# Loading v in four gated pieces, and q and k in eight pieces issued between the GpSimd sums, in an attention-and-feed-forward kernel

## The chip, the cores and the metric

The kernel runs on one core of a Trainium2 chip. The metric is device time in microseconds. A pass is one round of the main loop, for one of the eight batches; passes and units are counted from 0.

## The reference, cut to what matters

Inputs are q, k and v of shape (8, 8, 576, 64): batch, heads, sequence, head dimension. For each batch, groups of 18 sequence positions of q and k are averaged to 32 landmarks. Three softmax matrices are built from q, k and their landmarks, one is inverted by six Newton steps, and the product with v gives the attention output. The result goes through `((x @ w1) * (x @ w2)) @ w3 @ w_out`.

```python
q_lm = q.reshape(B, H, m, S // m, D).mean(axis=3)      # m = 32
k_lm = k.reshape(B, H, m, S // m, D).mean(axis=3)
A, Bm, C = sm(q, k_lm), sm(q_lm, k_lm), sm(q_lm, k)
Z = ...                                                # six times: Z = 2 * Z - Z @ Bm @ Z
attn = A @ Z @ C @ v
```

## The kernel before

The order of instructions on each engine is the order of the program. In pass b of the main loop TensorE makes the eight "up" units of batch b, interleaved with the steps of `attention` for batch b+1, then the "down" products of batch b. Meanwhile batch b+2 is prepared: its q and k are transposed by DMA, and GpSimd makes the landmark sums (`landmarks`), which end in the tile `parts`. The first step of `attention` for batch b+2 reads `parts` at the very end of pass b. q and k of batch b+3 are loaded in the same pass by GpSimd; these loads cast float32 to float16.

```python
def load_qk(st, b):
    qkn = pin.tile([128, 2, H, 384], FP16, name="qkn")
    for t, src in ((1, k), (0, q)):
        nc.gpsimd.dma_start(out=qkn[0:NP, t, :, :],
                            in_=src[b].rearrange("h (p r) d -> p h (r d)", p=NP))
...
def landmarks(st, t, eng=nc.gpsimd):
    ...
        eng.tensor_tensor(out=tr, in0=x[:, :, 0, :], in1=x[:, :, 1, :], op=ALU.add)
        eng.tensor_tensor(out=tr, in0=tr, in1=x[:, :, 2, :], op=ALU.add)
        ...                                              # two adds of thirds to o
        eng.tensor_copy(out=hi, in_=o)                   # hi and lo are halves of st["parts"]
        eng.tensor_tensor(out=lo, in0=o, in1=hi, op=ALU.subtract)

def attention(st, bank=None):
    ...
    psL = small()
    for i in range(2):                                   # hi, then lo
        nc.tensor.matmul(psL[:, :], iit.rearrange("p a d -> p (a d)"),
                         parts[:, i].rearrange("p t h l -> p (t h l)"),
                         start=(i == 0), stop=(i == 1))
    ...

for b in range(B):
    st = sts[b]
    ab = st["ab"] = pab.tile([128, 8, S], FP16, name="ab")
    if b + 2 < B:
        turn_all(b + 2)                                  # DMA transposes of q and k
        load_v(sts[b + 2], b + 2)                        # one load on the SP queue
    ...
    for j in range(8):
        up(st, j, 0)
        ...
        steps(at, ...)
        up(st, j, 1)                                     # VectorE writes ab[:, j, :]
    if b + 3 < B:
        load_qk(sts[b + 3], b + 3)
    if b + 2 < B:
        landmarks(sts[b + 2], 1)
        landmarks(sts[b + 2], 0)
    nxt = attention(sts[b + 2], acc) if b + 2 < B else iter(())
    ...                                                  # down products, rest of at
    steps(nxt)                                           # TensorE reads parts of b + 2
    at = nxt
```

The softmax here doesn't subtract the row's maximum and nothing guards it: scores larger than these inputs give would overflow.

## Time and profile before

| | before |
|---|---|
| time, median | 300.87 us (299.02 to 301.57, 3 runs; 300.5 with the run made beside the changed kernel) |
| TensorE (PE) busy | 276.5 of 299.0 us |
| GpSimd (POOL) busy | 135.6 us |
| one pass of the loop (passes 1 to 5) | 26.6 to 30.5 us |

From the page: the span, the busy time of each engine, the granted TensorE clock in 40 slices (9 is 90% or more), and the chain that ended last by engine.

```profile
span 299.0 us, 9452 instructions
...
PE 276.5 (92%) x4026; PEld 151.7 (51%) x4026; DVE 177.9 (59%) x454; ACT 124.3 (42%) x199; POOL 135.6 (45%) x176
...
PEclk9998999999979999999999999999999999999999
...
PE 73%; DMA 9%; DVE 9%; ACT 6%; issue 2%; POOL 0%; ACTq 0%; DVEq 0%
```

TensorE is busy nearly all the time and makes up 73% of the chain. GpSimd is on none of it (0%): what it does is done in time. GpSimd's timeline in pass 2 (start in us, duration, engine, line, operation):

```profile
146.18 0.72 POOL L262 TENSOR_TENSOR bmbd<-bmn,mask 128x256 f32<-128x256 f32 x1
146.84 0.82 POOL L71 DMA_DIRECT2D qkn<-in_k_dram  x1
147.65 0.77 POOL L71 DMA_DIRECT2D qkn<-in_q_dram  x1
148.43 1.65 POOL L166 TENSOR_TENSOR tr<-qkT 128x768 f32<-128x768 f16 x1
150.16 1.64 POOL L167 TENSOR_TENSOR tr<-tr,qkT 128x768 f32<-128x768 f32 x1
...
160.04 0.67 POOL L175 TENSOR_TENSOR parts<-o,parts 128x256 f16<-128x256 f32 x1
```

After the last product of the attention steps (line 262) GpSimd issues the two q/k loads, 0.82 and 0.77 us, and goes straight into twelve adds and copies that end at 160.04 + 0.67 = 160.7 us. This is the timeline of TensorE at the psL matmuls of passes 0, 1 and 2, which read that result:

```profile
108.68 0.64 PE L183 MATMUL small<-parts,iit 128*128 128x512 f16 x2
...
137.45 0.59 PE L183 MATMUL small<-parts,iit 128*128 128x512 f16 x2
...
164.12 0.61 PE L183 MATMUL small<-parts,iit 128*128 128x512 f16 x2
```

In pass 2 TensorE comes for `parts` at 164.1 us, 3.4 us after they are ready; in pass 1 it comes 5.6 us after. In pass 0 there is nothing between: the sums end at 108.9 us.

### The profile page before, as it was taken

The page shows a single profiled execution, that of the slowest core. Times are in us where ns is not written, and L with a number is a line of the kernel's source. Part 1 is how long each engine was busy: PE and PEld are TensorE (multiplying, and loading weights), DVE is VectorE, ACT ScalarE, POOL GpSimd, SP SyncE. Part 2 cuts the span into 40 slices and gives each one's busy share as a digit, 9 for nine tenths or more (in the row PEclk, how much of TensorE's full clock was granted, in tenths as well). Part 3 has the DMA queues.
Part 4 walks back from the last instruction along what each step waited for, and adds up shares of the span by engine and source line. Part 5 has one row for each costly group of instructions (what it writes and reads, how often), then busy time and mean ns, then how long its engine had stood idle before and what let it go on. Part 6 is the DMA issues. An engine that isn't in the chain of part 4 may idle for free.

```text
span 299.0 us, 9452 instructions
## 1 busy us (share of the span) xinstructions
PE 276.5 (92%) x4026; PEld 151.7 (51%) x4026; DVE 177.9 (59%) x454; ACT 124.3 (42%) x199; POOL 135.6 (45%) x176
## 2 busy tenths in 40 slices
PE   6867999999879989999999998999999999999993
PEld 3434555444446447445744663366447535743741
DVE  8922743465476576755765765476666655765720
ACT  2113442233344266236625741474167236525531
POOL 1608132270009958950994499039918940600000
PEclk9998999999979999999999999999999999999999
DMA  6999999939920948975996999379949632013124
GB/s 242 279 268 255 239 232 230 164 38 196 203 54 8 214 110 172 224 165 104 186 219 150 147 201 202 101 140 203 228 111 154 154 107 70 4 30 79 36 58 118
DMA packets 61385, 45.56 MB, mean 152 GB/s; under 512 B 34976, under 2 KB 53408, under 8 KB 61344
## 3 DMA queue, kind: packets, MB, share of 16 engines
q1 hardware_dynamic: 46896, 31.86, 47.1%
q0 software_dynamic: 13632, 11.54, 24.8%
q10 hardware_dynamic: 816, 1.57, 1.4%
q8 instruction: 31, 0.51, 0.7%
q14 instruction: 10, 0.08, 0.1%
HBM read 38.80 MB, written 9.44 MB: 161 GB/s over the span
## 4 chain that ended last, share of the span: by engine, by line
PE 73%; DMA 9%; DVE 9%; ACT 6%; issue 2%; POOL 0%; ACTq 0%; DVEq 0%
PE big L426 16%; PE acc L446 13%; PE big L446 10%; PE acc L490 9%; DMA qkn<-in_q_dram 6%; PE big L412 6%; DVE ab L432 4%; PE big L369 4%; ACT a_sb L430 3%; DMA wof<-in_moe_w_out_dram 2%; PE small L305 2%; PE acc L305 2%; PE big L477 2%; PE big L353 1%; PE big L224 1%
## 5 line engine op out<-in xcount | busy, mean ns | idle before, releaser
L426 PE MATMUL big<-ahat,gt 128*128 128x288 f16 x512 | 75.1, 288 | 3.1 <-ACT a_sb L430 1.9
L432 DVE TENSOR_TENSOR ab<-a_sb,big 128x576 f16<-128x576 f16 x64 | 47.9, 750 | 19.5 <-PE big L426 7.7
L430 ACT CAST a_sb<-big 128x576 f16<-128x576 f32 x64 | 41.0, 640 | 41.6 <-PE big L426 36.1
L426 PEld LDWEIGHTS <-gt 128*128 128x128 f16 x512 | 47.6, 98 | 20.7 <-issue 5.8
L235 POOL TENSOR_TENSOR t<-ect 96x384 f32<-96x384 f32 x16 | 16.0, 997 | 87.0 <-ACT ect L228 86.5
L490 PE MATMUL acc<-wsp,w3t 128*128 128x512 f16 x168 | 42.1, 384 | 1.6 <-DVE wsp L471 0.9
L446 PE MATMUL acc<-w,ab 128*128 128x512 f16 (+1 forms) x192 | 41.0, 382 | 0.1
L446 PEld LDWEIGHTS <-ab 128*128 128x128 f16 (+1 forms) x320 | 23.9, 100 | 32.4 <-issue 9.3
L446 PE MATMUL big<-w,ab 128*128 128x512 f16 x128 | 32.8, 381 | 0.0
L166 POOL TENSOR_TENSOR tr<-qkT 128x768 f32<-128x768 f16 x14 | 23.0, 1643 | 20.7 <-DMA qkT<-qkn 11.0
L418 DVE TENSOR_SCALAR gt<-big 128x1024 f16<-128x1024 f32 x16 | 19.5, 1224 | 17.7 <-PE big L412 17.7
L490 PEld LDWEIGHTS <-w3t 128*128 128x128 f16 x192 | 18.1, 100 | 20.1 <-issue 4.1
L452 ACT ACTIVATE o_sb<-acc 128x512 f32<-128x512 f32 x20 | 11.9, 597 | 37.4 <-PE acc L446 35.5
L167 POOL TENSOR_TENSOR tr<-tr,qkT 128x768 f32<-128x768 f32 x14 | 23.0, 1641 | 1.1
L416 ACT ACTIVATE gt<-big 128x1024 f16<-128x1024 f32 x16 | 16.4, 1024 | 8.6 <-PE big L412 8.6
L412 PE MATMUL big<-wup,zt 64*32 64x512 f16 x512 | 19.0, 380 | 0.8 <-DVE ahat L356 0.8
L483 DVE SCALAR_TENSOR_TENSOR w3t<-big,w3t 128x512 f16<-128x512 f32 x16 | 11.0, 689 | 14.1 <-ACT w3t L482 14.1
L452 ACT ACTIVATE o_sb<-big 128x512 f32<-128x512 f32 x16 | 9.6, 598 | 22.4 <-PE big L446 22.4
L482 ACT ACTIVATE w3t<-big 128x512 f16<-128x512 f32 x16 | 9.5, 597 | 19.9 <-PE big L477 19.5
L228 ACT ACTIVATE ect<-big 96x768 f32<-96x768 f32 x16 | 12.9, 807 | 2.9 <-PE big L224 2.4
L356 DVE TENSOR_TENSOR ahat<-eat,big 128x576 f16<-128x576 f16 x16 | 11.9, 749 | 1.8 <-PE big L353 1.8
L172 POOL TENSOR_TENSOR o<-o,tr 128x256 f32<-128x256 f32 x14 | 11.2, 799 | 1.1
(311 smaller groups left out, 358.9 us busy)
## 6 DMA issues: line engine op xcount, KB each, us to landing
vt<-in_v_dram SPq DMA_DIRECT2D x8, 1152.0 KB, 8.5
qkn<-in_k_dram POOLq DMA_DIRECT2D x8, 576.0 KB, 10.8
qkn<-in_q_dram POOLq DMA_DIRECT2D x8, 576.0 KB, 13.4
out_dram<-o_sb SPq DMA_DIRECT2D x24, 192.0 KB, 2.3
w3f<-in_moe_w_dram SPq DMA_DIRECT2D x6, 512.0 KB, 7.5
out_dram<-o_sb SPq DMA_DIRECT2D x24, 128.0 KB, 2.4
wup<-in_moe_w_dram POOLq DMA_DIRECT2D x4, 512.0 KB, 24.9
wof<-in_moe_w_out_dram ACTq DMA_DIRECT2D x3, 512.0 KB, 7.3
```

Of the source, the lines that this page charges most:

```text
L166: eng.tensor_tensor(out=tr, in0=x[:, :, 0, :], in1=x[:, :, 1, :], op=ALU.add)
L167: eng.tensor_tensor(out=tr, in0=tr, in1=x[:, :, 2, :], op=ALU.add)
L235: nc.gpsimd.tensor_tensor(out=t3[0:NP], in0=e[:, :, 0:3, :], in1=e[:, :, 3:6, :], op=ALU.add)
L412: nc.tensor.matmul(psG[32 * h:32 * h + 32, qd, :], zt[rs, i, h, :], wup[rs, h, w, fs], start=(i == 0), stop=(i == 1), tile_position=(64 * ...
L416: nc.scalar.activation(out=g[:, :, w, fs], in_=psG, func=AXF.Copy, scale=1.0 / ZS)
L418: nc.vector.tensor_scalar(out=g[:, :, w, fs], in0=psG, scalar1=1.0 / ZS, scalar2=None, op0=ALU.mult)
L426: nc.tensor.matmul(p[:, c, 0:HS], st["g"][:, qd, w, 128 * j:128 * j + 128], st["ahat"][qd][:, c, :], start=(qd == 0), stop=(qd == 1))
L430: nc.scalar.copy(out=st["a_sb"], in_=p[:, :, 0:HS])
L432: nc.vector.tensor_tensor(out=st["ab"][:, j, :].rearrange("p (c s) -> p c s", c=2), in0=st["a_sb"], in1=p[:, :, 0:HS], op=ALU.mult)
L446: nc.tensor.matmul(pso[o:o + sz, :], ab[:, j, s0:s0 + sz], w34[:, j, :], start=(j == 0), stop=(j == 7), tile_position=(0, o))
L452: nc.scalar.activation(out=o_sb, in_=pso[:, :], func=AXF.Copy, scale=1.0 / (X64 * X64))
L490: nc.tensor.matmul(psW[j][:, :], turned[j, c // 4][:, a, c % 4, :], wsp[:, b, c, :], start=(c == 0 and a + b == 0), stop=(c == 7 and a == 1))
```

## The change

The aim is to spread the loads over the pass. v comes in four pieces of two heads, and each may start only when an up unit is done: a one-column GpSimd copy reads `ab` and writes into the v tile, so that the load has to wait for it. q and k come in eight pieces of two heads, their issues set between the GpSimd sums.

```diff
--- before.py
+++ after.py
@@ -77,6 +77,23 @@
         nc.sync.dma_start(out=vt[0:NP], in_=v[b].rearrange("h (p r) d -> p h (r d)", p=NP))
         st["vt"] = vt
 
+    def load_v_piece(st, b, i, done):
+        if i == 0:
+            st["vt"] = pin.tile([128, H, 384], FP32, name="vt")
+        hs = slice(2 * i, 2 * i + 2)
+        nc.gpsimd.tensor_copy(out=st["vt"][0:NP, 2 * i, 0:1], in_=done)
+        nc.sync.dma_start(out=st["vt"][0:NP, hs],
+                          in_=v[b, hs].rearrange("h (p r) d -> p h (r d)", p=NP))
+
+    def qk_pieces(st, b):
+        st["qkn"] = pin.tile([128, 2, H, 384], FP16, name="qkn")
+        for t, src in ((1, k), (0, q)):
+            for i in range(4):
+                hs = slice(2 * i, 2 * i + 2)
+                nc.gpsimd.dma_start(out=st["qkn"][0:NP, t, hs, :],
+                                    in_=src[b, hs].rearrange("h (p r) d -> p h (r d)", p=NP))
+                yield
+
     def load_weight(t, w):
         for qd in range(2):
             nc.gpsimd.dma_start(out=wup[64 * qd:64 * qd + 64, :, t, :],
@@ -155,7 +172,7 @@
         return mask4, par, ones, eye2, iit, onesq, selc, lomask
 
 
-    def landmarks(st, t, eng=nc.gpsimd):
+    def landmarks(st, t, eng=nc.gpsimd, pieces=iter(())):
         if "parts" not in st:
             st["parts"] = pz.tile([128, 2, 2, H, 32], FP16, name="parts")
         for h0 in ((0,) if eng is nc.gpsimd else (0, 4)):
@@ -163,13 +180,17 @@
             hs = slice(h0, h0 + n)
             x = st["qkT"][:, t, hs, :, :]
             tr = pat.tile([128, n, NP], FP32, name="tr" + own, bufs=1)
+            next(pieces, None)
             eng.tensor_tensor(out=tr, in0=x[:, :, 0, :], in1=x[:, :, 1, :], op=ALU.add)
+            next(pieces, None)
             eng.tensor_tensor(out=tr, in0=tr, in1=x[:, :, 2, :], op=ALU.add)
+            next(pieces, None)
             t3 = tr.rearrange("p h (l g) -> p h l g", g=3)
             o = pat.tile([128, n, 32], FP32, name="o3" + own, bufs=1)
             hi, lo = st["parts"][:, 0, t, hs, :], st["parts"][:, 1, t, hs, :]
             eng.tensor_tensor(out=o, in0=t3[:, :, :, 0], in1=t3[:, :, :, 1], op=ALU.add)
             eng.tensor_tensor(out=o, in0=o, in1=t3[:, :, :, 2], op=ALU.add)
+            next(pieces, None)
 
             eng.tensor_copy(out=hi, in_=o)
             eng.tensor_tensor(out=lo, in0=o, in1=hi, op=ALU.subtract)
@@ -596,7 +617,6 @@
         ab = st["ab"] = pab.tile([128, 8, S], FP16, name="ab")
         if b + 2 < B:
             turn_all(b + 2)
-            load_v(sts[b + 2], b + 2)
         if b % 2 == 0:
             chunks = [[(b, ab, 128 * t, 128)] for t in range(4)]
         else:
@@ -607,12 +627,13 @@
             if b == 0 and j == 1:
                 landmarks(sts[1], 0, nc.vector)
             steps(at, (0, 0, 0, 1, 1, 1, 2, 2)[j] if b == 0 else 1)
+            if b + 2 < B and j > 3:
+                load_v_piece(sts[b + 2], b + 2, j - 4, st["ab"][0:NP, j - 1, st.get("t0", 0):st.get("t0", 0) + 1])
             up(st, j, 1)
-        if b + 3 < B:
-            load_qk(sts[b + 3], b + 3)
         if b + 2 < B:
-            landmarks(sts[b + 2], 1)
-            landmarks(sts[b + 2], 0)
+            pieces = qk_pieces(sts[b + 3], b + 3) if b + 3 < B else iter(())
+            landmarks(sts[b + 2], 1, pieces=pieces)
+            landmarks(sts[b + 2], 0, pieces=pieces)
         nxt = attention(sts[b + 2], acc) if b + 2 < B else iter(())
         hold = {}
         nd = 2 * len(chunks)
```

The order of instructions on TensorE, VectorE and ScalarE is the same in both kernels; only the GpSimd and SP streams differ.

## The prediction

> **What bounds the kernel now.** TensorE. The page's busy table has PE at 276.5 of 299.0 us (92%), and the chain that ended last is 73% PE. From about 95 us the kernel runs one batch in 27 to 30 us (windows table: PE busy 28.1 of 28.8, 26.0 of 26.9, 28.4 of 30.1). No load is waited for there: the list of waits, restricted to 110 to 270 us, shows nobody waiting for v, q, k or their transposes. So spreading v and q/k over time has almost nothing to win; the only DMA wait in it is ACT for output stores, 1.9 us in two places.
>
> **What the change does to engines.** The instruction order on PE, ACT and DVE is unchanged. On GpSimd, each of six batches gets four one-column copies (the gates), and batches 0 to 4 issue eight q/k loads instead of two, threaded between the landmark sums. GpSimd is in order, so (1) the sums of batch b+2 cannot start before the last gate, which waits for `ab` of unit 6, and (2) the issues sit inside the chain of sums. That chain ends in `parts`, which PE reads (psL matmul, line 183) at the batch boundary. PE is in order too: if `parts` is late, PE stands.
>
> **Costs, from the timeline of GpSimd before.** One batch's sums take 12.3 us (119.60 to 131.89). A 768-row q/k issue occupies GpSimd 0.77 to 0.82 us; a 256-row weight issue still 0.63. The Trainium skill ("DMA: Bandwidth & Descriptors", section "SWDGE vs HWDGE vs iDMA") says a GpSimd core computes these descriptors in software; the trace agrees that issuing occupies the engine. A line through the two sizes gives, as an estimate, 0.6 us for a 192-row piece, so 4.9 us for eight against 1.6 before. A gate I put at 0.3 us (the existing one-column gate copy took 0.43).
>
> **Slack, from the timelines.** New end of sums = end of `ab` 6 + 0.35 + 12.3 + 4.9:
> - batch 0: before, sums end at 108.9 and PE reads at 108.7 to 109.3, zero slack. `ab` 6 is early (92.9), so the delay is gates 1.0 + issues 3.3 = 4.3 us.
> - batch 1: 122.5 + 17.5 = 140.0, needed 137.45: 2.6.
> - batch 2: 151.3 + 17.5 = 168.8, needed 164.1: 4.7.
> - batch 3: 178.2 + 17.5 = 195.7, needed 194.5: 1.3.
> - batch 4: 208.3 + 17.5 = 225.8, needed 221.2: 4.7.
> - batch 5: no pieces, 247.5 against 249.8: none.
>
> Sum 17.6 us, all on the critical path since PE has nothing else in its order. A stall shifts everything after it, so the stalls add up.
>
> **Prediction: 318 us, 309 to 325; faster 0.04, within 2% 0.11, slower 0.85.**
>
> **What would show it.** New waits PE small L183-equivalent <- POOL `parts`, about five, sum 13 to 22 us, longest 4 to 5 us; POOL busy up by about 20 us, with 40 q/k issue records of about 0.6 us; PE busy time unchanged; batches 0, 2 and 4 stretched by 4 to 5 us, 1 and 3 by less; v pieces landing well before use; nobody waiting for qkT.
>
> **What would make it wrong.** The piece issue cost decides. If it scaled with rows (0.2 us each), the stalls shrink to about 4 us in batches 0, 2 and 4 together, and the time to 305 (within 2%). If it did not shrink at all (0.8), the sum is about 25 us. If late q pieces hold the transposes at the next batch's start so long that sums wait for them, it is worse than 325. It would be faster only if TensorE matmuls are slowed by bursts of DMA in a way this trace does not list as a wait.

## The result, and the profile after

| | before | after |
|---|---|---|
| time, median of 4 | 300.5 us (299.02 to 301.57) | 319.61 us (318.58 to 320.1) |
| ratio | | 1.0635, 95% interval 1.058 to 1.069 |
| PE busy | 276.5 us | 283.5 us |
| POOL busy | 135.6 us | 156.4 us |

A ratio is the mean time of one kernel's runs over that of the other's of the same rounds, so it is not quite the ratio of the medians quoted. Executions over 1.5% slower than the fastest of the same kernel are left out of the means. The page after, the same lines, the second line of the chain (by line of the program), and a group that is new in the list of costly ones (in a group: busy us, mean ns, then the idle time of its engine just before it and what ended most of that):

```profile
span 316.8 us, 9556 instructions
...
PE 283.5 (89%) x4026; PEld 155.0 (49%) x4026; DVE 178.5 (56%) x454; ACT 124.9 (39%) x199; POOL 156.4 (49%) x230
...
PEclk9989999999799989997999799999986999999998
...
PE 47%; POOL 27%; DMA 8%; DVE 8%; issue 5%; ACT 4%; ACTq 0%; DVEq 0%; POOLq 0%
PE big L447 15%; PE acc L511 9%; POOL qkn L93 8%; DMA qkn<-in_q_dram 5%; POOL tr L186 5%; POOL tr L184 5%; PE acc L467 5%; DVE ab L453 4%; PE big L467 4%; POOL o L192 2%; DMA wof<-in_moe_w_out_dram 2%; PE big L433 2%; POOL o L191 2%; PE small L326 2%; ACT a_sb L451 2%
...
L204 PE MATMUL small<-parts,iit 128*128 128x512 f16 x16 | 6.6, 432 | 17.1 <-POOL parts L195 13.0
```

GpSimd now holds 27% of the chain, with the q/k issues (line 93) as its largest item, and TensorE waits 13.0 us for `parts`. The clock row has four slices at 7 or 6, where the row before had one. The timeline of GpSimd in pass 2 of the changed kernel:

```profile
151.88 0.73 POOL L283 TENSOR_TENSOR bmbd<-bmn,mask 128x256 f32<-128x256 f32 x1
...
157.13 0.18 POOL L84 CAST vt<-ab 96x1 f32<-96x1 f16 x1 [1.39 <-DVE ab L453]
157.37 0.69 POOL L93 DMA_DIRECT2D qkn<-in_k_dram  x1
158.07 1.65 POOL L184 TENSOR_TENSOR tr<-qkT 128x768 f32<-128x768 f16 x1
159.66 0.66 POOL L93 DMA_DIRECT2D qkn<-in_k_dram  x1
160.34 1.65 POOL L186 TENSOR_TENSOR tr<-tr,qkT 128x768 f32<-128x768 f32 x1
...
173.61 0.66 POOL L196 TENSOR_TENSOR parts<-o,parts 128x256 f16<-128x256 f32 x1
```

The last gate (line 84) waited for unit 6 until 157.1 us, 4.5 us after GpSimd had done everything else that came before it (151.88 + 0.73 = 152.6). Then each issue takes 0.66 to 0.69 us of GpSimd, and the sums end 16.9 us after the first issue began, where the two issues and the same sums took 13.9 us before (146.84 to 160.71). And the timeline of TensorE at the same matmuls as shown before; the number in brackets is its idle time and who ended it:

```profile
109.90 0.59 PE L204 MATMUL small<-parts,iit 128*128 128x512 f16 x1 [2.79 <-POOL parts L195]
...
141.54 0.38 PE L204 MATMUL small<-parts,iit 128*128 128x512 f16 x1 [1.46 <-POOL parts L195]
...
173.58 0.38 PE L204 MATMUL small<-parts,iit 128*128 128x512 f16 x1 [3.62 <-POOL parts L195]
174.33 0.38 PE L204 MATMUL small<-parts,iit 128*128 128x512 f16 x1 [0.37 <-POOL parts L196]
```

In pass 2 TensorE now stands 3.62 us for the first and 0.37 us for the second of the two matmuls. The five waits come to 13.0 + 1.4 = 14.4 us by the list of waits. To see the rest of the 19 us, take the interval from one start of the psB matmuls, just behind psL, to the next. The first interval ends behind the psL of pass 0, the next behind that of pass 1, and so on; the last has no q/k pieces in its pass and no wait at its end. "Fill" and "v on VectorE" are experiments told below.

| interval, us | 0 | 1 | 2 | 3 | 4 | 5 | sum |
|---|---|---|---|---|---|---|---|
| before | 23.3 | 28.8 | 26.6 | 30.5 | 26.6 | 28.8 | 164.5 |
| after | 27.5 | 31.2 | 32.2 | 32.1 | 31.2 | 30.2 | 184.4 |
| fill (e5) | 27.6 | 30.8 | 30.8 | 31.2 | 30.8 | 28.8 | 180.0 |
| v on VectorE (e12) | 23.6 | 28.8 | 26.6 | 28.8 | 26.6 | 28.8 | 163.0 |

Every interval that ends in a wait grew. Interval 3 grew by only 1.6 us, less than its wait of 1.9, because the kernel before had a standstill of 1.0 us of its own there (told under e12). Interval 5 grew by 1.4 us although nothing waits for `parts` in it. The windows table of the changed kernel behind the wait of pass 2 shows what may have done it (window, its length, PE busy and instructions, granted clock, DMA share, GB/s):

```profile
core 0: us, PE busy (x), PEclk, DMA share, GB/s
173.50:174.50 1.00, 0.55 (x2) 1.00 1.27 188
174.50:175.50 1.00, 1.00 (x5) 0.54 1.84 197
175.50:176.50 1.00, 1.00 (x13) 0.50 1.65 87
176.50:177.50 1.00, 1.00 (x6) 0.50 1.34 230
177.50:178.50 1.00, 1.00 (x14) 0.75 1.28 287
178.50:179.50 1.00, 0.92 (x8) 1.00 0.72 137
```

About a microsecond after the wait the granted clock falls to 0.50 for some 3 us. This is found behind four of the five waits, for 3 to 7 us; behind the fourth it stays at 1.00.

### The profile page after: what moved, and what is told of

Read it like the earlier page. It is cut to its first block, busy times and chain, and to the rows that moved or that the text cites. A ratio compares the mean times of both kernels' runs of the same rounds, so it can differ in the third digit from the quotient of the medians.

```text
span 316.8 us, 9556 instructions
## 1 busy us (share of the span) xinstructions
PE 283.5 (89%) x4026; PEld 155.0 (49%) x4026; DVE 178.5 (56%) x454; ACT 124.9 (39%) x199; POOL 156.4 (49%) x230
## 4 chain that ended last, share of the span: by engine, by line
PE 47%; POOL 27%; DMA 8%; DVE 8%; issue 5%; ACT 4%; ACTq 0%; DVEq 0%; POOLq 0%
PE big L447 15%; PE acc L511 9%; POOL qkn L93 8%; DMA qkn<-in_q_dram 5%; POOL tr L186 5%; POOL tr L184 5%; PE acc L467 5%; DVE ab L453 4%; PE big L467 4%; POOL o L192 2%; DMA wof<-in_moe_w_out_dram 2%; PE big L433 2%; POOL o L191 2%; PE small L326 2%; ACT a_sb L451 2%
## 5 line engine op out<-in xcount | busy, mean ns | idle before, releaser
L447 PE MATMUL big<-ahat,gt 128*128 128x288 f16 x512 | 80.9, 304 | 2.9 <-ACT a_sb L451 1.3
L447 PEld LDWEIGHTS <-gt 128*128 128x128 f16 x512 | 49.7, 103 | 25.2 <-issue 8.5
L84 POOL CAST vt<-ab 96x1 f32<-96x1 f16 x24 | 4.3, 182 | 42.1 <-issue 21.8
L204 PE MATMUL small<-parts,iit 128*128 128x512 f16 x16 | 6.6, 432 | 17.1 <-POOL parts L195 13.0
L211 DVE TENSOR_TENSOR qbd<-lm,par 128x512 f16<-128x512 f16 x8 | 5.5, 692 | 19.4 <-ACT lm L209 19.4
```

The source lines that it names most:

```text
L447: nc.tensor.matmul(p[:, c, 0:HS], st["g"][:, qd, w, 128 * j:128 * j + 128], st["ahat"][qd][:, c, :], start=(qd == 0), stop=(qd == 1))
```

## The experiments

The theory on trial: GpSimd time ahead of the end of the sums is the whole cost. The gates hold the sums back, the issues make them longer, both use up the same slack, and TensorE then waits and loses clock. Rivals: the pieces hurt as transfers, by landing late or by contention; or the two parts of the change cost something each, and add.

### e1: only the v pieces

```diff
-            pieces = qk_pieces(sts[b + 3], b + 3) if b + 3 < B else iter(())
-            landmarks(sts[b + 2], 1, pieces=pieces)
-            landmarks(sts[b + 2], 0, pieces=pieces)
+            load_qk(sts[b + 3], b + 3)          # whole, where they were before
+            landmarks(sts[b + 2], 1)
+            landmarks(sts[b + 2], 0)
```

> Only the gated v pieces; q and k go back to two whole loads ahead of the sums. Theory (GpSimd order: the sums start late because of the gate on unit 6, and grow by the issues between them, until they run past the slack before TensorE reads parts): the sums end 14.2 us after ab of unit 6 instead of 17.8, which is within the slack in batches 1 and 3, about 1.1 us past it in 2 and 4, about 0.4 in 0. So 2.6 us of waits for parts plus at most 2 for a lowered TensorE clock: 303.5 us, 301.5 to 305.5. Rival A (the pieces hurt as transfers: q/k landing late or contending with other transfers): q/k whole again, so before's time, 300.5, unless v is to blame. Rival B (the two parts of the change add up, the gate being the larger): 310 or more.

Measured: 302.09 us (301.52 to 303.22), ratio to before 1.003 (0.9992 to 1.0068). Its list of waits has 2.6 us for `parts`, as reckoned. The gates alone cost nothing that can be told from noise.

### e2: only the q/k pieces

```diff
         if b + 2 < B:
             turn_all(b + 2)
+            load_v(sts[b + 2], b + 2)
-            if b + 2 < B and j > 3:
-                load_v_piece(...)
```

> Only the q/k pieces between the sums; v is one ungated load as before. Theory: sums start when they did before and take 3.7 us longer (eight issues of 0.66 us against two of 0.80). Batch 0 had no slack: 3.7 us; batch 1 had 5.5 and batch 3 7.2: nothing; batches 2 and 4 had 3.4: 0.3 each. 4.3 us of waits plus about 1.7 of lowered clock: 306 us, 303.5 to 308. The two halves alone then make about 9 us of the 19: the rest is there only when both eat the same slack. Rival A (the pieces as transfers): close to the whole 319. Rival B (additive): 310.

Measured: 307.69 us (307.45 to 308.49) in three runs, a fourth, slow one of 312.29 left out; ratio 1.0229 (1.0189 to 1.0269). That is at the upper end of what was expected. The waits for `parts` were 2.9 us where 4.3 were reckoned; three other standstills, 3.9 us in all, were not reckoned: 1.0 us at 57 us, ahead of the loop, 2.4 in pass 1 and 0.6 in pass 3. The one in pass 1:

```profile
124.54 1.16 PE L447 MATMUL big<-ahat,gt 128*128 128x288 f16 x8
128.06 0.40 PE L390 MATMUL big<-sz__1715,tz__1716 32*32 32x96 f32 x16 [2.36 <-issue]
```

2.36 us pass with no releaser that the profile shows. In the weight loads the gap falls behind the first of the sixteen loads of this group, so nothing new was to be waited for. The queues of the DMA engines in the microsecond from 125 us, where it starts (packets, MB, share of 16 engines):

```profile
q0 software_dynamic: 147, 0.11, 72.0%
q1 hardware_dynamic: 66, 0.08, 40.9%
q8 instruction: 1, 0.02, 8.5%
```

An instruction block crosses just then, while q/k pieces and the whole v load fill the engines to 113% by this count. The Trainium skill ("Runtime: NRT & Kernel Launch", section "Instruction fetch mechanics") says that instructions are refilled in 16 KiB blocks by DMA while the engine works on the previous block, and calls the cost mostly hidden. Here it may not be hidden. e10 tests whether the whole v load has a part in it; what speaks against it is told under e9 and e12.

The two halves alone cost 1 and 7 us by the medians, together 19. So they do not add, and the reason is the slack: in passes 1 to 4 either half alone stays within it or passes it by little.

### e3: v pieces with their gates on VectorE

```diff
-        nc.gpsimd.tensor_copy(out=st["vt"][0:NP, 2 * i, 0:1], in_=done)
+        nc.vector.tensor_copy(out=st["vt"][0:NP, 2 * i, 0:1], in_=done)
```
(with e1's whole q/k loads)

> As the v-only kernel, but the one-column gate copies run on VectorE, just behind the ab that they wait for; v still arrives in four gated pieces. Theory: GpSimd is as before, so no wait for parts, and v in pieces wins nothing: 300.5 us, 299.5 to 302.5 (24 small copies on VectorE). Rival A (v pieces hurt as transfers or their issue blocks the output stores behind them): as the v-only kernel. Rival C (spreading v is a gain that the GpSimd cost hides): below 299.

Measured: 299.44 us (299.24 to 301.85), ratio 0.9967 (0.9919 to 1.0015). No wait for `parts` on GpSimd. With GpSimd left alone, v in pieces costs nothing, and may win a little; e12 says which.

### e4: GpSimd adds in the places of six issues

```diff
 def qk_pieces(st, b):
-    for t, src in ((1, k), (0, q)):
-        for i in range(4):
-            ... nc.gpsimd.dma_start(...)          # eight pieces
-            yield
+    load_qk(st, b)                               # two whole loads
+    yield
+    spare = pat.tile([128, 4, NP], FP32, name="trv", bufs=1)
+    for i in range(6):
+        nc.gpsimd.tensor_tensor(out=spare[:, :, 0:64], in0=selc[:, 0, :, 0:64],
+                                in1=selc[:, 0, :, 64:128], op=ALU.add)
+        yield
```

> The changed kernel with q and k as two whole loads and, in the places of the other six issues, six GpSimd adds of about 0.65 us that nobody reads. Theory (GpSimd time in the chain of sums is all that the pieces cost): as the changed kernel, 319.6 us, 317 to 322. Rival A (what costs is the pieces' transfers): as the v-only kernel, about 303.

Measured: 321.72 us (319.69 to 323.59), ratio 1.0687. The adds as a group, and TensorE's wait:

```profile
L93 POOL TENSOR_TENSOR trv<-selc 128x256 f32<-128x256 f16 x30 | 20.0, 667 | 0.0
```

```profile
PE small L204 <- POOL parts L195: 14.5, 5, 4.0
```

Adds of 0.667 us do to TensorE what issues of 0.66 us did (13.0 us in the changed kernel), with q and k loaded whole. (Two whole issues and six adds are some 0.3 us more per pass than eight piece issues, which fits the slightly longer waits.) So it is the time on GpSimd, not the transfers. For q and k this falsifies the rival of late or contending pieces as the main cost; for v, e3 and e10 do.

### e5: TensorE kept busy in its waits

```diff
         psL = small()
+        for _ in range(fill):                    # 10, 5, 13, 5, 13, 0 in passes 0 to 5
+            nc.tensor.matmul(psL[:, :], iit.rearrange("p a d -> p (a d)"), w34[:, 0, :],
+                             start=True, stop=True)
```

> The changed kernel with TensorE kept busy through most of each wait for parts: 10, 5, 13, 5 and 13 matmuls of 512 columns (about 0.22 to 0.24 us each) into the bank that psL overwrites, before the two psL matmuls of batches 0 to 4. In the changed kernel's trace the granted clock is 0.50 for 3 to 7 us behind four of the five waits. Theory (the part of the 19 us that the 14.4 us of waits do not explain is this lowered clock): the clock stays at 1.00 at these places and the time falls by about 4 us, to 315.5 (313 to 317.5), although work was added. Rival (the low clock costs nothing, because after the wait the other engines bound): 319.6.

Measured: 316.8 us (315.44 to 318.44), ratio 1.0526 (1.0473 to 1.058), where the changed kernel had 1.0635. A kernel with 46 useless matmuls more is some 3 us faster. The windows table behind the wait of pass 2:

```profile
170.00:180.00 10.00, 8.51 (x77) 1.00 1.11 171
180.00:190.00 10.00, 9.52 (x234) 1.00 0.42 118
```

```profile
PE small L207 <- POOL parts L195: 2.9, 5, 0.7
```

The clock stays at 1.00 and what is left of the wait for the first half of `parts` is small (second fence, list of waits). In the table of intervals, interval 5 is back at 28.8 us from 30.2: there is no wait in it, so its 1.4 us were the low clock alone. The sum of intervals falls by 184.4 - 180.0 = 4.4 us. With the 14.4 us of waits that is 18.8 of the 19.9 us by which the sums before and after differ.

### e10: the whole change, gates on VectorE

The edit is that of e3, made in the changed kernel.

> The whole change, only with the gate copies on VectorE. Then the sums do not wait for unit 6: as in the q/k-only kernel they grow by 3.7 us and only batch 0 is late by about 2.9 us, with about 1.7 us of lowered clock behind it. The q/k-only kernel came out at 308.1, with 2.9 us of waits for parts; its trace has one more standstill of TensorE, 2.36 us at 125.7 us, inside a group of matmuls, just where a 16 KB instruction block crosses while the whole v load and q/k pieces fill the DMA engines. Theory (a late instruction block behind the bulk v load): with v in pieces it goes, 304.5 us (303 to 306). Rival (something of the q/k pieces that does not depend on v): 307 to 309.

Measured: 302.38 us (301.03 to 303.57), ratio 1.003 (0.9987 to 1.0073), better than expected. One wait for `parts` on GpSimd is left, in pass 0, 2.5 us for its first half and 0.2 for the second, with a clock of 0.50 for some 3 us behind it; no standstill without a releaser. From its list of waits:

```profile
PE small L204 <- POOL parts L195: 2.5, 1, 2.5
```

This kernel has every piece that the change has, and v's still stand in SyncE's queue behind their gates. Against e2 it differs only in v, and is 5.3 us faster by the medians, of which the three standstills of e2's trace, 3.9 us, are the part that the traces name. That an instruction block came late because of the bulk load is not shown: it is one trace of each, and e9 speaks against it.

### e6: sixteen q/k pieces

```diff
-            for i in range(4):
-                hs = slice(2 * i, 2 * i + 2)
+            for i in range(8):
+                hs = slice(i, i + 1)
```
(two of them in each place)

> The changed kernel with sixteen q/k pieces of one head, two in each place. Theory (a cost per issue: 0.66 us for 192 rows, 0.80 for 768, so about 0.64 for 96): eight more issues are 5.1 us in each of five chains of sums with no slack left, 25.6 us, and up to 5 us of lowered clock behind the longer waits: 348 us, 344 to 353. Rival (a cost per byte or per row): 320.

Measured: 337.02 us (336.43 to 338.28), ratio 1.1201. The direction holds, the size was over-reckoned. The issue groups of this kernel and, in the second fence, of the changed kernel:

```profile
L93 POOL DMA_DIRECT2D qkn<-in_k_dram x40 | 20.7, 522 | 0.2
```

```profile
L93 POOL DMA_DIRECT2D qkn<-in_k_dram x20 | 13.4, 668 | 0.2
```

A one-head piece takes 0.52 us, not the 0.64 of the straight line; I did not foresee that. A one-head piece has an access pattern with one dimension less, which may be what makes it cheaper to issue; no run tests it. With 0.52, a pass has 16 x 0.52 - 8 x 0.66 = 3.0 us more, 15 us in five; the time rose by 17.4 us over the changed kernel and the waits for `parts` from 14.4 to 28.3 us.

### e7: four q/k pieces

As e6, with slices of four heads: two pieces of k and two of q.

> The changed kernel with four q/k pieces of four heads in the first places instead of eight. 192 rows took 0.66 us to issue and 96 rows 0.52, 768 rows 0.80, so about 0.71 for 384: the chain of sums gets 2.4 us shorter than in the changed kernel, whose five waits were 2.95, 1.8, 4.0, 1.9 and 3.8 us. Theory: 0.5, 0, 1.6, 0 and 1.4 remain, 3.5 us, and at most 2 us of lowered clock: 305 us, 303 to 307.5. Rival (a cost that goes with the bytes in pieces): 319.

Measured: 308.4 us (308.12 to 308.63), ratio 1.0223: a miss by a microsecond at the upper end. An issue took 0.70 us, as reckoned, but the waits shrank from 14.4 to 5.6 us only, not to 3.5: the chain got about 1.9 us shorter per pass, not 2.4 (pass 0: 2.95 to 1.04 us of wait, pass 2: 3.99 to 2.17). A likely reason: two dependent adds back to back have a pause of 0.08 us between them (150.16 after 148.43 + 1.65 in the timeline of before), and an issue set between them fills it, so taking it out saves less than its length. From start to start the first two adds are 1.73 us apart before and 2.27 with an issue between them (160.34 - 158.07): 0.54 us more for an issue of 0.66. e8 points the same way.

### e8: the eight issues ahead of the sums

```diff
+            steps(pieces, 9)
             landmarks(sts[b + 2], 1, pieces=pieces)
```

> The changed kernel with all eight q/k issues ahead of the sums instead of between them. Theory (their sum counts, not their places): 319.6 us, 317.5 to 321.5. Rival (it is the breaking up of the sums, or the late landing of the last pieces, that costs): 310 or less.

Measured: 322.9 us (322.47 to 324.24), ratio 1.0734, above the expected range by 1.4 us. The wait for the first half of `parts`, 13.0 us in the changed kernel:

```profile
PE small L204 <- POOL parts L195: 15.2, 5, 4.1
```

Their place among the sums does not make the cost. On the contrary, placed between the sums they are slightly cheaper: from the first issue to the end of the sums pass 1 takes 17.4 us here (127.24 to 144.61) and 16.9 us in the changed kernel (125.32 to 142.23).

### e9: the eight issues behind the sums

```diff
             pieces = qk_pieces(sts[b + 3], b + 3) if b + 3 < B else iter(())
-            landmarks(sts[b + 2], 1, pieces=pieces)
-            landmarks(sts[b + 2], 0, pieces=pieces)
+            landmarks(sts[b + 2], 1)
+            landmarks(sts[b + 2], 0)
+            steps(pieces, 9)
```

> The changed kernel, gates on GpSimd and all eight q/k pieces kept, but the eight issues put behind the two sums instead of into them. Theory (only what stands ahead of the end of the sums costs): the sums end 12.5 us after ab of unit 6, at or before the time TensorE wants parts in every batch, so no waits of more than 0.3 us for parts, although GpSimd does the same work: 301 us, 299.5 to 303. The 5.2 us of issues then stand ahead of the next batch's first sums of exponentials, which have some slack. Rival (GpSimd is simply given too much work, or pieces that land late hold the next transposes): 310 or more.

Measured: 302.32 us (301.58 to 303.58), ratio 1.0026 (0.9976 to 1.0077). The gates are on GpSimd, all 40 pieces are there with 0.63 to 0.65 us each, and no wait for GpSimd's `parts` is left. The same work on the same engine, moved behind the last thing that somebody waits for, costs nothing that can be told from noise. The rest that its trace shows is three standstills of TensorE: 1.1 us at 174.7 us and 1.5 at 206.0 without a releaser, and 1.5 at 119.1, behind the first of sixteen weight loads as in e2, which the list of waits puts down to a copy on ScalarE that had ended 0.8 us before. TensorE, and what the DMA engines moved in each fortieth of the microsecond from 206 us:

```profile
207.46 0.42 PE L447 MATMUL big<-ahat,gt 128*128 128x288 f16 x2 [1.48 <-issue]
```

```profile
GB/s 0 10 10 0 20 10 10 10 0 10 10 10 10 10 10 10 10 0 20 10 10 0 10 11 10 10 10 10 10 51 236 307 256 287 297 307 266 276 317 297
```

v comes in pieces here, the DMA engines stand nearly still in the first half of the standstill, and the last instruction block had crossed at 204 to 205 us. So neither a bulk v load nor DMA engines that are full when it begins are needed for such a standstill.

### e11 and e12: is there anything to win?

e12 is e3 again, in five rounds. e11 adds eight matmuls as in e5, ahead of the psL of batch 1 in the first pass, where TensorE waits 2.4 us for sums made on VectorE, in all kernels here but e11 itself.

> The kernel with v pieces gated on VectorE again, now in five rounds, to say whether v in pieces wins anything over before at all: 299.4 against 300.85 was within noise. If the standstill of TensorE of about 1 us at an instruction block (181.8 us in the trace of before, none in this kernel's) is the difference, 299.5, ratio 0.995 to 0.998; if it was noise, 300.9.

> A try for a better kernel: v pieces gated on VectorE, q and k whole, and eight matmuls that nobody reads ahead of the psL matmuls of batch 1 in the first pass, where TensorE waits 2.4 us for sums made on VectorE and the granted clock is 0.50 for about 3 us after. If the low clock costs there, about 1 us under the same kernel without them (run beside it), 298.5; if not, the same.

Measured: e12 299.38 us (298.31 to 300.52), ratio to before 0.9931 (0.9887 to 0.9975), slightly below the expected 0.995. e11 297.73 us (296.85 to 299.56), ratio 0.9878 (0.9834 to 0.9923), 1.6 us under e12 by the medians where 1 was expected. The granted clock at that place in e11, then in e12, from their windows tables:

```profile
83.00:84.00 1.00, 0.90 (x7) 1.00 0.00 0
84.00:85.00 1.00, 1.00 (x16) 1.00 0.11 25
```

```profile
83.00:84.00 1.00, 0.90 (x4) 0.50 0.00 0
84.00:85.00 1.00, 1.00 (x6) 0.50 0.00 0
```

So v in pieces does win something, 0.7%, once the gates are off GpSimd; and keeping the clock up at one more wait seems to win about half a per cent more. Both are clear of noise against before, and below 2%; between the two the intervals overlap, so the half per cent is less sure than the traces of the clock. Where e12 wins is seen in the table of intervals, one trace of each: all are as before, but interval 3 is 28.8 instead of 30.5 us. In before, TensorE stood there inside a group of matmuls:

```profile
181.43 0.35 PE L369 MATMUL big<-sz__3047,tz__3045 32*32 32x96 f32 x4
182.81 0.39 PE L369 MATMUL big<-sz__3047,tz__3045 32*32 32x96 f32 x12 [1.02 <-issue]
```

An instruction block crosses at 180 to 181 us, while the two whole q/k loads fill the DMA engines to 134% by the count used under e2. None of the traces of e3, e10, e11 and e12 has this standstill. But in the kernel before, blocks also cross at 125, 154 and 210 us, with the engines at 126 to 142%, and TensorE does not stand there; and e9, with v in pieces, has the three told above. So full engines at a crossing do not suffice, and the cause stays open.

## Why the prediction was right

**TensorE bound, with no slack in its order: right.** Every wait for `parts` showed up as time: intervals 0, 2 and 4 grew by 4.2, 5.6 and 4.6 us, lowered clock included (4 to 5 predicted), 1 and 3 by 2.4 and 1.6 (less, as predicted).

**The gate holds the sums back and the issues lengthen them: right, shown by e4, e9 and e10.** e4 put adds for issues and lost the same; e9 and e10 kept all pieces and moved what stood in the way, and lost nothing measurable. The estimate of 0.6 us for an issue was 0.66 in the trace; the gate was 0.18 us, not 0.3.

**Not additive: implied by the sums of the prediction, shown by e1 and e2.** 1 and 7 us alone, 19 together.

**The size was right partly because two errors cancelled.** Predicted waits by pass were 4.3, 2.6, 4.7, 1.3 and 4.7 us, 17.6 in all. Measured were 2.95, 1.8, 4.0, 1.9 and 3.8, 14.4 in all: the gates were cheaper, and the issues between the sums filled some of the pauses between the adds. Left out altogether was the clock: "PE busy time unchanged" was wrong, it rose by 7.0 us. e5 puts 3 us (by the ratios) to 4.4 us (by the intervals) on the lowered clock. I had the Trainium skill at hand ("TensorE: Matmul & The Clock Gate", section "What's actually happening": the clock halves when the array is found idle in a free-running window of about 3.4 us) and did not ask whether the predicted waits would trip it. The trace agrees with the halving: 0.50. But in pass 1 it followed waits of 1.83 us in all, about half of such a window.

**"Spreading v has almost nothing to win": nearly right.** e12 shows 0.7%, and it came at a place that the list of waits puts under no DMA, as a standstill without a releaser.

**The other marks.** POOL busy rose by 20.8 us (about 20 predicted), 40 issue records of 0.66 us (0.6), the longest wait 4.0 us (4 to 5). v pieces landed in 3.2 us and nobody waited for them, nor, in the loop, for transposed q and k.

What stays open: what the standstills without a releaser are: in e2 and before they coincide with an instruction block and full DMA engines, but other such blocks passed without one, and the two in e9 began with the engines nearly idle; and why the clock stayed up behind the wait of pass 3.

## What to carry to other kernels

Before putting work on an engine that is off the critical path, look up when its results are wanted and how long before that they are ready: the busy share says nothing of it, and two changes that each fit into the slack need not fit together. An issue from GpSimd is GpSimd time, nearly the same for a quarter of the bytes, so many small loads belong behind the last result that somebody waits for, and a copy that waits belongs on an engine where it holds up no such result, as here the gates on VectorE. And a wait of TensorE can cost more than its length, since the clock may halve for some microseconds after it.

## What the Trainium skill lacked or had wrong

- "DMA: Bandwidth & Descriptors", section "Anatomy of one DMA — SWDGE (gpsimd) path", calls descriptor generation a small, variable part of a DMA's fixed cost, and section "Issuing engines are not separate DMA queues" calls the issue time usually small relative to the DMA. It gives no time, by size, that an issue occupies GpSimd. Here it was 0.52 us for 96 rows (one dimension less), 0.66 for 192, 0.70 for 384 and 0.77 to 0.82 for 768, and it was this time behind the gates' hold-up, not the transfer, that cost 19 us.
- "TensorE: Matmul & The Clock Gate", section "Why this matters for your kernels", advises no idle gaps of TensorE over about 3 us. Here waits of 1.46 and 0.37 us, close together, were followed by 0.50 of the clock in pass 1, and waits of 1.49 and 0.37 us in pass 3 were not; after 3.62 us it was 0.50 for 3 to 7 us, and after the single wait of 2.40 us in the first pass of e12 for about 3 us. A gap under 3 us was not safe here.
- No page says that filling a wait with matmuls that nobody reads can pay: e5 against the changed kernel, 1.0526 against 1.0635 of before's time.
- "Runtime: NRT & Kernel Launch", section "Instruction fetch mechanics", calls the cost of crossing an instruction block mostly hidden. The traces have standstills of TensorE of 1.0 and 2.36 us at blocks that crossed while the DMA engines were full; the link is not shown, since three such blocks passed without one in the kernel before, and e9 has standstills of 1.1 and 1.5 us that began with the engines nearly idle.
- No page says that an issue set between two dependent GpSimd adds costs less than its length: eight ahead of the sums made the chain 17.4 us, eight between them 16.9.
